# One transfer for four heads of q, and k and v of the first batch on all 128 partitions

## The chip, the cores and the metric

The kernel runs on one core of a Trainium2 chip. A core has five engines that each work through a queue of their own in order: TensorE (PE, matmuls; the loading of its weights is shown as PEld), VectorE (DVE), ScalarE (ACT), GpSimd (POOL) and SyncE (SP), which in this kernel issues all transfers. The metric is the device time of one execution in microseconds, and the kernel before and the changed one are compared by it.

## The reference

Linear attention feeds two layers with activations, the second with weights of its own; all data is float32.

```
q, k, v: [4 batches, 8 heads, 576 tokens, 64]
q_s = exp(q - max over 64), divided by its sum over the 64      # softmax over a head's width
k_s = exp(k - max over tokens), divided by its sum over tokens  # softmax over the 576 tokens
kv  = k_s^T v                  # 64 x 64 for each batch and head
x   = q_s kv                   # to [2304 tokens, 512]
h   = x @ w_in;  x2  = (h * sigmoid(1.702 h)) @ w_out           # 512 -> 2048 -> 512
h   = x2 @ w_in2; out = (h * tanh(softplus(h))) @ w_out2
```

## The kernel before

**Stages.** The tokens are cut into five blocks of 512, 512, 512, 384 and 384 (`SIZES`). For the first three blocks the first layer is done directly: for each of 16 column blocks of `w_in` a group of 12 matmuls makes `h` (`gemm_in`, L1029), ScalarE and VectorE make the activation `g` of it, and 12 matmuls add it to four accumulators `acc` (`gemm_out`, L1098). From 330 us on the rest of the first layer and the second one run as products of 256 to 384 columns with fewer multiplications (L1322, L1661, L1552). Each float32 operand is split into a high and a low part, so a product takes three matmuls (`SPLIT`). The 32 weight blocks of the first layer are loaded into four buffers `raw`, decoded on ScalarE and VectorE (L414 or L418, L450, L461, L474) and split (L404 or L405 for the high part, L397 for the low one) into `wi` and `wo`.

**Attention** is done block by block (`attention(blk)`). `q_soft` takes half of the heads: it loads four heads of q (for block 0 into `qr`, for later blocks into `qt` with `q_load`), and VectorE and ScalarE make the softmax. `q_turn` transposes two heads on TensorE (L918), a copy `qT` is taken (L928), and `x_part` multiplies it by the pair's `kv32` (L948); ScalarE and VectorE write the high and low part of x (`xt<-at`, L903 and L908). One `unit` is a pair of heads, and each batch has four. For the first batch it is `k_first`: TensorE turns k so that tokens lie along a row (L692), VectorE takes the maximum (L705), ScalarE the exponential with its sum (L720), TensorE turns it back (L731), a copy goes to `kt` (L740), and `k_kv` multiplies by v (L768). Later batches take `k_later`. In block 1 and later the units use the bank `at0`, and q and x the bank `at1`. k lies on 96 partitions with six tokens of each head (`KP`, `KC`):

```python
kt = [ap.tile([KP, 2, KC, D], F32, name=f"kt{i}") for i in range(2)]
vd += [sp.tile([KP, 2, KC, D], F32, name=f"vd{i}") for i in range(1, NHP)]
```

**Order.** Every piece of work is recorded as an operation with costs (`plan.op`), and `Plan` makes the order in which each engine's instructions are written. It plays the operations through by their costs with random noise on their urgency, `PASSES` times from `SEED`, and takes the best order. It also writes filler transposes of the identity (`idle`, L1696; 40 in the kernel before) where it sees TensorE idle ahead of the first matmul of h. So a changed cost or seed changes the order all through the program.

## Time and profile before

| | |
|---|---|
| median of 3 runs | 817.04 us (816.63 to 819.48) |
| the profiled execution | 817.37 us, of which its span 815.5 us |
| PE, DVE, ACT busy | 99%, 81%, 55% of the span |
| granted clock of TensorE | 1.000, the level of 2.4 GHz |
| transfers | 208.58 MB, 78.3% of 16 DMA engines' span |

The span runs from the first to the last instruction; launch and end lie around it. Matmuls are pipelined, so a busy PE counts time in which one waits inside the array as well.

### The profile page before, as it was taken

How to read it: one execution, taken by the hardware profiler on the slowest of the kernel's cores; microseconds unless marked ns; L12 is line 12 of the kernel's file. 1: busy time of each engine (PE TensorE's matmuls, PEld its weight loads, DVE VectorE, ACT ScalarE, POOL GpSimd, SP SyncE). 2: the span in 40 equal slices, each digit the busy share in tenths (PEclk: the TensorE clock that was granted, in tenths of full speed). 3: DMA queues.
4: the chain of work that ended last, by engine and by line, in shares of the span. 5: the costliest groups of instructions: out<-in, count | busy, mean ns of one | idle time of the engine just before them, and what ended most of it. 6: DMA issues, size and time to landing. Idle time of an engine off the chain costs nothing.

```text
span 815.5 us, 14362 instructions
## 1 busy us (share of the span) xinstructions
PE 806.4 (99%) x5104; PEld 734.5 (90%) x5104; DVE 657.9 (81%) x1272; ACT 452.2 (55%) x860; POOL 16.9 (2%) x22
## 2 busy tenths in 40 slices
PE   8999899999999999999999999999999999999998
PEld 7788678877788888999999999999999999999997
DVE  6999887799986787777779879978777996677963
ACT  5999765355665456655556545555344563344542
POOL 0000000010000001000000000002000010000000
PEclk9999999999999999999999999999999999999999
DMA  9799765457878788887798898999589897777752
GB/s 241 227 274 294 228 216 171 169 171 231 228 249 286 237 277 279 272 333 267 264 305 288 278 331 285 295 319 392 173 273 295 291 309 223 227 250 265 270 190 60
DMA packets 126984, 208.58 MB, mean 256 GB/s; under 512 B 37568, under 2 KB 87488, under 8 KB 126912
## 3 DMA queue, kind: packets, MB, share of 16 engines
q1 hardware_dynamic: 126912, 207.66, 78.3%
q8 instruction: 41, 0.67, 0.3%
q14 instruction: 31, 0.25, 0.1%
HBM read 152.57 MB, written 55.05 MB: 255 GB/s over the span
## 4 chain that ended last, share of the span: by engine, by line
PE 87%; DVE 2%; ACT 1%; DMA 1%; issue 0%; ACTq 0%; SPq 0%; DVEq 0%
PE acc L1552 22%; PE at L1322 18%; PE acc L1098 13%; PE h L1029 12%; PE h L1322 10%; PE acc L1661 5%; PE h L1661 2%; PE at L948 2%; PE at L768 1%; PE at L918 1%; DMA raw<-in_moe_w_out_dram 1%; DVE dec L474 0%; PE h L1552 0%; DVE dec L397 0%; ACT dec L450 0%
## 5 line engine op out<-in xcount | busy, mean ns | idle before, releaser
L1098 PE MATMUL acc<-g,wo 128*128 128x512 f32 x576 | 145.7, 396 | 0.0
L1029 PE MATMUL h<-xt,wi 128*128 128x512 f32 x576 | 144.7, 396 | 0.0
L1552 PE MATMUL acc<-wi,second 128*128 128x256 f32 x1116 | 137.5, 283 | 0.0
L1552 PEld LDWEIGHTS acc<-wi,second 128*128 128x128 f32 x1116 | 135.6, 192 | 0.0
L1098 PEld LDWEIGHTS acc<-g,wo 128*128 128x128 f32 x576 | 106.6, 188 | 23.0 <-issue 1.0
L1029 PEld LDWEIGHTS h<-xt,wi 128*128 128x128 f32 x576 | 106.2, 188 | 23.0 <-issue 1.1
L1322 PE MATMUL at<-xt,wi 128*128 128x384 f32 x612 | 119.1, 335 | 0.1
L1322 PEld LDWEIGHTS at<-xt,wi 128*128 128x128 f32 x612 | 106.8, 188 | 3.0 <-DVE gt L1374 0.4
L1344 ACT ACTIVATE quad<-quad 128x384 f32<-128x384 f32 x96 | 50.3, 526 | 89.1 <-DVE quad L1374 88.7
L405 ACT ACTIVATE second<-quad 128x384 fp32r<-128x384 f32 x125 | 64.8, 523 | 49.2 <-PE acc L1552 44.7
L397 DVE TENSOR_TENSOR second<-quad,second 128x384 fp32r<-128x384 f32 x126 | 71.4, 571 | 14.8 <-ACT second L405 14.3
L1322 PE MATMUL h<-xt,wi 128*128 128x384 f32 x348 | 66.0, 334 | 0.0
L397 DVE TENSOR_TENSOR quad<-quad 128x384 f32<-128x384 f32 x96 | 53.1, 556 | 13.9 <-ACT quad L1344 12.2
L1322 PEld LDWEIGHTS h<-xt,wi 128*128 128x128 f32 x348 | 60.8, 188 | 0.0
L1552 PE MATMUL acc<-wi,g 128*128 128x256 f32 x372 | 48.2, 283 | 0.0
L1322 PE MATMUL at<-wi,wi 128*128 128x384 f32 x246 | 48.2, 334 | 0.0
L1552 PEld LDWEIGHTS acc<-wi,g 128*128 128x128 f32 x372 | 46.2, 192 | 0.0
L474 DVE CUSTOM_DVE_ANT_0 dec<-raw,dec 128x1024 uint16<-128x1024 uint16 x64 | 43.7, 686 | 2.0 <-ACT raw L414 0.5
L405 ACT ACTIVATE raw<-dec 128x512 fp32r<-128x512 f32 (+1 forms) x61 | 35.4, 598 | 16.5 <-DVE dec L397 10.7
L1322 PEld LDWEIGHTS at<-wi,wi 128*128 128x128 f32 x246 | 43.3, 188 | 0.7
L405 ACT ACTIVATE g<-gt 128x512 fp32r<-128x512 f32 (+1 forms) x42 | 26.3, 626 | 30.9 <-PE acc L1098 29.0
L1052 ACT ACTIVATE gt<-h 128x512 f32<-128x512 f32 x41 | 24.4, 594 | 32.4 <-PE h L1029 32.1
(179 smaller groups left out, 1179.2 us busy)
## 6 DMA issues: line engine op xcount, KB each, us to landing
wi<-combos SPq DMA_DIRECT2D x96, 512.0 KB, 5.1
wi<-outs SPq DMA_DIRECT2D x76, 512.0 KB, 5.6
raw<-in_moe_w_in_dram SPq DMA_DIRECT2D x32, 512.0 KB, 5.2
raw<-in_moe_w_out_dram SPq DMA_DIRECT2D x32, 512.0 KB, 4.8
combos<-raw SPq DMA_DIRECT2D x32, 512.0 KB, 3.6
outs<-raw SPq DMA_DIRECT2D x32, 256.0 KB, 3.2
wi<-combos SPq DMA_DIRECT2D x32, 256.0 KB, 4.9
combos<-raw SPq DMA_DIRECT2D x24, 256.0 KB, 3.8
```

What stands on the lines that cost most here:

```text
L397: return lambda: engine.tensor_tensor(out=out(), in0=in0(), in1=in1(), op=op)
L405: (ACT, act_ns(n), lambda: nc.scalar.activation(out=out(), in_=in_(), func=AF.Copy), False),
L474: dve(512, [rl], [da], lambda: nc.vector.tensor_tensor(out=a, in0=a, in1=lo_w, op=ALU.add), pair=True)
L768: nc.tensor.matmul(out=ps3[j * D : (j + 1) * D, 0:width], lhsT=of[:, j, c, :], rhs=w[:, j, c, :], start=c == 0, stop=c == KC - 1,)
L948: nc.tensor.matmul(out=part(ps[:, 0:nb]), lhsT=kv32[hp], rhs=part(qT32[hp % 2][:, 0:nb]), start=True, stop=True)
L1029: nc.tensor.matmul(out=h(), lhsT=w_mm(fc, 0, a, cc), rhs=x_of(t)[:, cc, b, :], start=cc == 0 and i == 0, stop=cc == NCC - 1 and i == 2,)
L1052: act(nb, [hk, ("tables",)], [tk], lambda: nc.scalar.activation(out=t, in_=h, func=AF.Tanh, scale=0.851), psum=True)
L1098: nc.tensor.matmul(out=acc[dm][:, 0:nb], lhsT=w_mm(fc, 1, a, dm), rhs=g_of(n)[:, b, :], start=fc == 0 and i == 0, stop=fc == NFC - 1 and i ...
L1322: nc.tensor.matmul(out=bank_of(key)[:, 0:NB], lhsT=wt(fc, 0)[:, w : w + P], rhs=operand(k, b)[:, cc, :], start=cc == 0 and i == 0, stop=cc ...
L1344: nc.scalar.activation(out=t(), in_=t(), func=AF.Mish if n >= NPR else AF.Gelu_apprx_sigmoid)
L1552: nc.tensor.matmul(out=bank_of(banks[c])[:, at_ : at_ + 256], lhsT=slot(pr, a)[:, c * P : c * P + P], rhs=rhs(b), start=pr == 0 and i == 0 ...
L1661: nc.tensor.matmul(out=o, lhsT=w_mm(2 * n + j, 1, a, dm), rhs=g_tile(n, j)[:, b, lo:hi], start=n == 0 and j == 0 and i == 0 and (c < 4 or ...
```

## The change

k and v of the first batch lie on 128 partitions, 64 for each of the two heads, with nine tokens on each; the products of a unit of the first batch work on 64 by 64 tiles, 18 instead of 12 of them, and turning back is a matmul with the identity, no transpose. For block 1 and later, `q_load` issues one transfer for four heads where it issued four (the pieces of 256 bytes stay). The planner's costs, seed and number of passes change, and so do the places of some combinations of weights in the second half (`EARLY`, `LATE_RIGHTS`, `LATER`, `RIGHTS`, `FIRST`).

```diff
-    PASSES = 30
-    SEED = 2
+    PASSES = 20
+    SEED = 948
...
-    FREE = {DMA: 1700.0, POOL: 2200.0, PE: 1750.0}
+    FREE = {DMA: 2500.0, POOL: 2200.0, PE: 1750.0}
...
-    TURNS = ((0, 4), (4, 6))
+    HC = 9
+    HP = S // HC
+    TURNS = ((0, 6), (6, 9))
...
-    kt = [ap.tile([KP, 2, KC, D], F32, name=f"kt{i}") for i in range(2)]
+    kfull = [ap.tile([P, 2 * KC * D], F32, name=f"kt{i}") for i in range(2)]
+    kt = [t[0:KP, :].rearrange("p (j c d) -> p j c d", j=2, c=KC) for t in kfull]
...
+    kd = [t[:, 0 : HC * D] for t in kfull]
+    kd += [sp.tile([P, HC * D], F32, name=f"kt{i}") for i in range(2, NHP)]
...
+    def by_head(a, hp):
+
+        return a[0, 2 * hp : 2 * hp + 2].rearrange("h (p c) d -> (h p) (c d)", c=HC)
...
                 for c in range(lo, hi):
                     for j in range(2):
+                        o = slice(j * D, (j + 1) * D)
                         nc.tensor.matmul(
-                            out=ps[i][j * D : (j + 1) * D, (c - lo) * KP : (c - lo + 1) * KP],
-                            lhsT=t[:, j, c, :],
-                            rhs=ident[0:KP, 0:KP],
+                            out=ps[i][o, (c - lo) * HP : (c - lo + 1) * HP],
+                            lhsT=t[o, c * D : (c + 1) * D],
+                            rhs=ident[o, o],
...
-                    nc.tensor.transpose(
-                        ps[i][0:KP, (c % 3) * P : (c % 3 + 1) * P], turned[h][:, n * KP : (n + 1) * KP], ident
-                    )
...
+                        nc.tensor.matmul(
+                            out=ps[i][o, c * D : (c + 1) * D],
+                            lhsT=turned[i][o, c * HP : (c + 1) * HP],
+                            rhs=ident[o, o],
...
-            for j in range(4):
-                dma(
-                    (hi - lo) * 256,
-                    begun,
-                    [("qt", j, i)] if len(cuts) > 1 else q_keys([j]),
-                    lambda j=j, lo=lo, hi=hi: qt[lo // NCT : hi // NCT, :, j, :],
-                    lambda j=j, b=b, s=s, n=hi - lo: q[b, 4 * half + j, s : s + n, :].rearrange("(p c) d -> p c d", c=NCT),
-                    slow=2,
-                )
+            dma(
+                (hi - lo) * 1024,
+                begun,
+                [("qt", j, i) for j in range(4)] if len(cuts) > 1 else q_keys(range(4)),
+                lambda lo=lo, hi=hi: qt[lo // NCT : hi // NCT],
+                lambda b=b, s=s, n=hi - lo: q[b, 4 * half : 4 * half + 4, s : s + n, :].rearrange(
+                    "h (p c) d -> p c h d", c=NCT
+                ),
+                slow=1.5,
+            )
```

In the changed kernel the lines stand 4 to 23 lower: L692, L731, L768, L1696 and L1029 are L700, L740, L780, L1719 and L1052 there; L397, L404, L418, L461, L474 and L908 are L401, L408, L422, L465, L478 and L931; L414, L450, L903 and L928 are L418, L454, L926 and L951.

**TensorE at the start of the program, the first two units.** A row is a run of equal instructions; `kt_116` and `kt_117` are k of the first two pairs, `stage` the exponentials, `h_107<-ident` fillers. Before:

```order
L1696 MATMUL h_107<-ident 128x128 x18
L692 MATMUL acc_99<-ident,kt_116 64x96 x8
L692 MATMUL acc_100<-ident,kt_116 64x96 x4
L692 MATMUL acc_101<-ident,kt_117 64x96 x8
L692 MATMUL acc_102<-ident,kt_117 64x96 x4
L1696 MATMUL h_107<-ident 128x128 x5
L731 MATMUL acc_99<-ident,stage 96x128 x3
L731 MATMUL acc_100<-ident,stage 96x128 x3
L1696 MATMUL h_107<-ident 128x128 x7
L768 MATMUL acc_99<-gt,kt_116 64x64 x12
```

Now:

```order
L1719 MATMUL h_107<-ident 128x128 x12
L700 MATMUL acc_99<-ident,kt_116 64x64 x12
L700 MATMUL acc_100<-ident,kt_116 64x64 x6
L1719 MATMUL h_107<-ident 128x128 x4
L700 MATMUL acc_102<-ident,kt_117 64x64 x6
L700 MATMUL acc_101<-ident,kt_117 64x64 x12
L1719 MATMUL h_107<-ident 128x128 x24
L740 MATMUL acc_99<-ident,stage 64x64 x12
L740 MATMUL acc_100<-ident,stage 64x64 x6
L740 MATMUL acc_102<-ident,stage 64x64 x6
```

Each product has half as many instructions again, the way back to tokens goes from 6 to 18, and the longest run of fillers now stands between turning k and turning it back.

**VectorE between the second and the fourth x part of block 0** (`xt<-at` is the low part of x; `wi_69` and `wi_70` are the second and third tile of `w_in`). Before:

```order
L908 TENSOR_TENSOR xt<-at_112,xt 128x512
...
L805 TENSOR_SCALAR kv_3_123<-acc_101,rs 64x64
L397 TENSOR_TENSOR wi_69<-dec_93,wi_69 128x512
L675 TENSOR_TENSOR pmt<-pmt 96x128
L418 TENSOR_SCALAR raw_91<-raw_91 128x512
L675 TENSOR_TENSOR pmt<-pmt 96x128
L908 TENSOR_TENSOR xt<-at_111,xt 128x512
L474 ISA dec_94<-raw_90,dec_94 128x1024
L461 TENSOR_SCALAR dec_92<-dec_92 128x512
L908 TENSOR_TENSOR xt<-at_112,xt 128x512
L404 CAST wi_70<-dec_94 128x512
```

Now:

```order
L401 TENSOR_TENSOR wi_69<-dec_93,wi_69 128x512
L682 TENSOR_TENSOR pmt<-pmt 96x128
L422 TENSOR_SCALAR raw_91<-raw_91 128x512
L682 TENSOR_TENSOR pmt<-pmt 96x128
L422 TENSOR_SCALAR raw_88<-raw_88 128x512
L465 TENSOR_SCALAR dec_94<-dec_94 128x512
L478 ISA dec_94<-raw_90,dec_94 128x1024
L408 CAST wi_70<-dec_94 128x512
L422 TENSOR_SCALAR raw_89<-raw_89 128x512
L401 TENSOR_TENSOR wi_70<-dec_94,wi_70 128x512
L931 TENSOR_TENSOR xt<-at_111,xt 128x512
L931 TENSOR_TENSOR xt<-at_112,xt 128x512
```

The third tile of `w_in` is now decoded to its end, and two later raw tiles are begun, ahead of the third and fourth x part. Over the whole list ahead of the fourth x part (rows not shown here) the counts are: L401 for `wi` three for two, L408 two for none, L422 four for two, L465 three for four, and none for two of L805, whose work ScalarE does now.

**ScalarE in block 1, from the first copy of qT to the x part that follows** (`raw` are weights that a transfer brings, `wo_437` and `wo_541` the last four tiles of `w_out`). Before:

```order
L928 ACTIVATE qT_0_124<-at_112 128x512
L414 ACTIVATE raw_88<-raw_88 128x512
L450 ACTIVATE dec_93<-raw_88 128x512
L414 ACTIVATE raw_89<-raw_89 128x512
L450 ACTIVATE dec_94<-raw_89 128x512
L797 ACTIVATE kv_0_120<-at_111,rs 64x64
L903 ACTIVATE xt<-at_112 128x4x16
```

Now:

```order
L951 ACTIVATE qT_0_124<-at_112 128x512
L409 ACTIVATE wo_541<-dec_92 128x512
L454 ACTIVATE dec_94<-raw_89 128x512
L768 ACTIVATE kt_116<-kt_116 96x768
L926 ACTIVATE xt<-at_112 128x4x16
```

One conversion of a raw weight stands there for four, and the exponential of the block's first k pair has come in. On TensorE the two rows ahead of this and the work behind it read now as follows; before, the row of `mcol` and the product with `vt` (L752 and L768) stood far ahead of the q turn and just ahead of it:

```order
L941 MATMUL at_112<-ident,qt 128x128 x4
L765 MATMUL at_111<-ident,mcol 96x128
L1121 MATMUL acc_99<-g,wo_83 128x512 x3
L1121 MATMUL acc_100<-g,wo_83 128x512 x3
L971 MATMUL at_112<-qT_0_124,kv_0_120 128x4x16
L1121 MATMUL acc_101<-g,wo_83 128x512 x3
L1121 MATMUL acc_102<-g,wo_83 128x512 x3
L790 MATMUL at_111<-vt,kt_116 64x66 x12
L941 MATMUL at_112<-ident,qt 128x128 x4
```

SP's queue now holds all raw loads of the first layer ahead of the loads of block 1's second half of q; before, the last raw load stood behind them.

## Rows read from the trace of the kernel before

**Rows 1.** The chain that ended last, shares by engine.

```profile
PE 87%; DVE 2%; ACT 1%; DMA 1%; issue 0%; ACTq 0%; SPq 0%; DVEq 0%
```

**Rows 2.** Stretches (us): length, each engine busy (instructions), clock, DMA share, GB/s.

```profile
5.50:30.60 25.10, 24.13 (x277) 19.64 (x277) 23.64 (x53) 20.17 (x49) 0.00 (x0) 1.00 0.98 254
...
85.00:96.00 11.00, 8.63 (x62) 6.40 (x62) 9.25 (x21) 9.48 (x20) 1.44 (x1) 1.00 0.83 219
...
340.00:815.50 475.50, 471.36 (x3178) 462.36 (x3176) 364.66 (x702) 232.44 (x448) 7.35 (x4) 1.00 0.80 269
```

**Rows 3.** PE's waits, 34 to 340 us: total, times, longest.

```profile
PE at L918 <- DVE xt L908: 1.7, 1, 1.7
PE at L948 <- ACT qT L928: 0.6, 1, 0.6
```

**Rows 4.** PE in order of time, 28 to 36 us: start, length, run.

```profile
32.52 3.69 PE L1029 MATMUL h<-xt,wi 128*128 128x512 f32 x15
```

**Rows 5.** All engines in order of time, 0 to 40 us.

```profile
5.51 1.22 DVE L859 TENSOR_REDUCE qs<-qr 128x16 f32<-128x1024 f32 x1 [5.51 <-DMA qr<-in_q_dram]
...
6.58 4.11 PE L692 MATMUL acc<-ident,kt 96*64 96x96 f32 x48 [0.97 <-DMA kt<-in_k_dram]
...
11.22 0.82 PE L731 MATMUL acc<-ident,stage 128*96 128x128 f32 x6
...
12.73 0.92 PE L768 MATMUL acc<-gt,kt 96*64 96x64 f32 x24
...
14.92 1.21 PE L692 MATMUL acc<-ident,kt 96*64 96x96 f32 x24
...
29.89 0.68 DVE L908 TENSOR_TENSOR xt<-at,xt 128x512 fp32r<-128x512 f32 x1
```

**Rows 6.** Stretches of one microsecond, columns as in the second group.

```profile
3.00:4.00 1.00, 1.00 (x7) 1.00 (x6) 0.00 (x0) 0.00 (x0) 0.00 (x0) 1.00 1.04 357
...
13.00:14.00 1.00, 1.00 (x28) 0.93 (x23) 1.00 (x3) 1.00 (x5) 0.00 (x0) 1.00 1.09 257
```

**Rows 7.** PE's instructions of the units: ns (min/median/max, or busy us and mean).

```profile
L692 PE MATMUL acc<-ident,kt x96: 246/332/421, 6.6 to 19.2; 96*64 96x96 f32 x96
...
L731 PE MATMUL acc<-ident,stage 128*96 128x128 f32 x24 | 3.4, 276 | 0.0
L768 PE MATMUL acc<-vd,kt 96*64 96x64 f32 x72 | 2.7, 225 | 0.0
```

**Rows 8.** VectorE's instructions by shape, 0 to 34 us: busy us, mean ns.

```profile
L397 DVE TENSOR_TENSOR wi<-dec,wi 128x512 fp32r<-128x512 f32 x3 | 2.0, 667 | 0.0
...
L461 DVE TENSOR_SCALAR dec<-dec 128x512 int32<-128x512 int32 x5 | 2.1, 417 | 0.0
...
L418 DVE TENSOR_SCALAR raw<-raw 128x512 int32<-128x512 uint32 x3 | 1.3, 418 | 0.0
...
L805 DVE TENSOR_SCALAR kv<-acc,rs 64x64 f32<-64x64 f32 x2 | 0.6, 292 | 0.2
...
L404 DVE CAST wi<-dec 128x512 fp32r<-128x512 f32 x1 | 0.4, 412 | 0.0
```

**Rows 9.** ScalarE in order of time, 66 to 96 us.

```profile
71.51 0.83 ACT L755 ACTIVATE kt<-kt 96x768 f32<-96x768 f32 x1
...
88.64 0.58 ACT L928 ACTIVATE qT<-at 128x512 f32<-128x512 f32 x1
89.11 0.67 ACT L414 ACTIVATE raw<-raw 128x512 int32<-128x512 uint32 x1
...
91.42 0.68 ACT L414 ACTIVATE raw<-raw 128x512 int32<-128x512 uint32 x1 [1.09 <-DMA raw<-in_moe_w_out_dram]
...
92.75 0.21 ACT L903 ACTIVATE xt<-at 128x64 fp32r<-128x64 f32 x1
```

**Rows 10.** SP's issues in order of time, 84 to 97.5 us.

```profile
86.70 3.46 SPq L388 DMA_DIRECT2D qt<-in_q_dram  x4
...
96.93 0.52 SPq L388 DMA_DIRECT2D raw<-in_moe_w_out_dram  x1
```

More of the change, by code (lines that the diff above doesn't have):

```diff
@@ L443, in decoded @@
             src = w_ap[m][1][fc * P : (fc + 1) * P, :]
-        dma(P * 4096, pace, [rl, rh], lambda: dst, lambda: src, slow=1.2 if io == 0 else 1)
+        dma(P * 4096, pace, [rl, rh], lambda: dst, lambda: src, slow=1.15)
         if signed:
@@ L698, in turn @@
                         )
-            pe(180 * (hi - lo), [kk], [keys[i]], turn, whole=True)
+            pe(122 * (hi - lo), [kk], [keys[i]], turn, whole=True)
             dve(
-                (hi - lo) * KP,
+                (hi - lo) * HP,
                 [keys[i]],
                 [("km", u, i)],
-                lambda i=i, n=(hi - lo) * KP: nc.vector.reduce_max(out=km[:, u, i : i + 1], in_=ps[i][:, 0:n], axis=AX.X),
+                lambda i=i, n=(hi - lo) * HP: nc.vector.reduce_max(out=km[:, u, i : i + 1], in_=ps[i][:, 0:n], axis=AX.X),
             )
@@ L759, in k_kv @@
         kk = ("kt", k_tile(u))
-        t = kt[k_tile(u)]
-        width = D if first else D + 2
+        t = None if first else kt[k_tile(u)]
         def mm():
-            of = t.rearrange("p j c d -> p (j c d)").rearrange("p (c j d) -> p j c d", j=2, c=KC) if first else t
-            w = vd[u] if first else vt
+            if first:
+                for c in range(HC):
+                    for j in range(2):
+                        o = slice(j * D, (j + 1) * D)
+                        nc.tensor.matmul(
+                            out=ps3[o, 0:D],
+                            lhsT=kd[u][o, c * D : (c + 1) * D],
+                            rhs=vd[u][o, c * D : (c + 1) * D],
+                            start=c == 0,
+                            stop=c == HC - 1,
+                        )
+                return
             for c in range(KC):
@@ L777, in k_kv @@
         rk = ("rs", u % NHP)
-        pe(720, [kk] + [kk + (j,) for j in range(2)] + v_keys(u), [key3], mm, whole=True)
+        pe(1090 if first else 720, [kk] + [kk + (j,) for j in range(2)] + v_keys(u), [key3], mm, whole=True)
         if first:
```

60 lines of the change are left out of this document (31 added, 29 removed).

## The prediction

> **What bounds the kernel now.** I read the chain that ended last first: 87% of it is TensorE, and no other engine has more than 2% [rows 1]. Then the stretches [rows 2]: from 340 us on PE is busy for 471.36 of 475.50 us and the list of PE's waits is empty there, so whatever makes that part begin later or earlier moves the end by the same amount. Of all that lies between 34 and 340 us PE's waits name only two, 1.7 us for an x part on VectorE and 0.6 us for a qT copy on ScalarE, 2.3 us together [rows 3]; the stretch 85 to 96 us is where they lie (PE busy 8.63 of 11 us [rows 2]). So two places can give time: the opening, up to the moment when PE starts the groups of h without a break (it has 15 matmuls in one run from 32.52 us; the last 12 of them, the group of the third w_in tile, start 0.78 us on, at 33.3 us [rows 4]; such matmuls start 0.23 us apart, 15 in 3.69 us with the length of the last), and the two waits near 90 us, 2.3 us.
>
> In the opening VectorE is the engine that is full: it begins at 5.51 us, when the first half of q has landed, starts the fourth and last x part at 29.89 us [rows 5], and is busy for 23.64 of the 25.10 us between [rows 2]. PE is not full there: it runs 40 filler transposes of the identity.
>
> **The change part by part.** *The order of the first loads.* k of the first pair now stands ahead of q. Before, the first transposes of k wait until 6.58 us [rows 5], behind 512 KB of q and 288 KB of k. How fast the two move is in two rows: 357 GB/s in the microsecond that moves q (128 partitions), 257 in one that moves only k and v (96 partitions) [rows 6]. Without q ahead of it (524 KB / 357 = 1.5 us) and at the rate of q (295 KB: 1.15 us at 257, 0.83 at 357, so 0.3 less) k lands near 6.54 - 1.8 = 4.7 us. That does not start VectorE earlier: its first instruction is now the maximum over six transposed token blocks. The transposes of k from 6.58 us took 4.11 us for 48 records and those at 14.92 us 1.21 for 24 [rows 5]; less the length of the last record (0.42 at the most and 0.25 at the least [rows 7]) that is 0.15 and 0.08 us for a pair of records (two heads side by side), although the column of the granted clock says 1.00 (2.4 GHz) throughout. At the early pace 12 pairs of 64 columns take 12 x 0.15 x 64/96 = 1.2 us, so with 0.2 for the hand-over VectorE starts at about 6.1 us, 0.6 later than before.
>
> *128 partitions for k and v.* By the two rates eight transfers save 8 x 0.3 = 2.6 us of the DMA stream. [...] I take no gain from the faster transfers in the sum, since VectorE is full from 5.5 us and never starved by a landing after the first (bounds: 0 and -1.8 us, the earlier landing of k).
>
> *More matmuls for the same tokens.* A unit (pair of heads) has 18 instead of 12 in each of its products, and the way back is 18 matmuls where there were 6 transposes. Pairs of 64 columns: k times v has 24 records in 0.92 us [rows 5], of which the last alone is 0.22 [rows 7], so 0.058 us a pair; 18 matmuls are 18 such pairs, 1.05 us. Before: turning 12 x 0.08 = 0.98, back 6 x 0.109 = 0.65 (0.82 us for six [rows 5], less the last one's 0.27 [rows 7], over 5 spacings), k times v 0.70. So a unit costs PE 0.07 + 0.40 + 0.35 = 0.8 us more, four units 3.3. For the first two units the fillers in the row give way. For units 2 and 3 the way back and k times v, 2 x 0.75 = 1.5 us, stand between the first x part and the groups of h, where the built order has one filler instead of five, and PE has little else to give up.
>
> *VectorE's list ahead of the fourth x part.* In the built order it has one wi subtract (0.667), two casts (0.412) and two low-half conversions (0.418) more than before, and one shift (0.417) and two kv scalings (0.292) fewer [rows 8]: 0.67 + 0.82 + 0.84 - 0.42 - 0.58 = 1.3 us, or 1.0 since neighbours overlap by some 0.08 us each. This is decoding done ahead, not lost, but PE waits for the x part, not for it. ScalarE's second copy of a unit has 192 columns in place of 384; I count that as nothing, since the x part waits for VectorE's list.
>
> *Sum for the opening.* By VectorE: start +0.6, list +1.0, and it can win back at most the 1.46 us that it was idle: between +0.1 and +1.6 us, the middle +0.9. By PE: up to +1.5, less its one or two short gaps. Both say about **+1.0 us**; ends 0 and +2.1 (the upper if the early pace of PE outlasts the 24 fillers: 3.5 us more at half pace is 1.75 us of work on the way to kv of the first unit, of which the fillers hide some 0.7).
>
> *The two waits near 90 us.* Before, ScalarE has four conversions of raw weights between the first qT copy of block 1 (88.64 us) and the x part that frees PE's bank (92.75 us); one of them waits 1.09 us for its weights [rows 9]. The engine takes its queue in order, so the x part waits with it, and PE with the x part. Behind those weights four loads of q, a head each, hold the issuing queue for 3.46 us, and the last weights are only issued at 96.93 us [rows 10]. In the new order one raw conversion and the exponential of k stand between the qT copy and the x part, and all raw loads stand ahead of that half of q. From the end of the qT copy to that of the x part: a weight copy and a conversion at 0.6 each, k's exponential at 0.75 and the x part 0.2, together 2.15 us ([rows 9], less 0.08 of overlap each), while PE has the x product itself, 6 matmuls (1.36) and k times v (0.7): over 2.1 us. So the 1.7 should go and the 0.6 mostly: **-2.1 us**; ends -2.3 and, if the new chain waits as the old did, 0.
>
> *q in one transfer.* The pieces stay 256 bytes, so the bytes' time stays; 56 issues become 14. SP is no engine that PE waits for, and outside block 1 no wait on q is on PE's list [rows 3]: 0, with the gain at block 1 counted above. If one issue of four heads takes more than the four did (0.9 us each near 87 us [rows 10]), SP holds the next loads back; the blocks after the first have nothing near it that PE lacks. The rest of the reordering (pairing of weights, late combinations) I price at 0, between -0.5 and +0.5: PE has no wait there that could go.
>
> Sum: +1.0 - 2.1 = -1.1 us. The profiled execution took 817.37 us (span 815.50); less 1.1 is 816.3. Its time is 0.33 over the median of the runs, 817.04, so **815.9 us** by the median.
>
> **The rivals.**
> *The wait moves.* In the new order the maximum of block 1's first k pair comes back to PE only two rows after the q turn, and k must then pass VectorE (768 columns, at the pace of 1.22 us for 1024 [rows 5]: 0.9 us) and ScalarE (0.83 [rows 9], behind a weight that may not have landed) before k times v, six rows on. With three hand-overs at 0.15 that is 2.2 us; 12 matmuls (2.7 us) and an x product cover it. One landing as late as the 1.09 us of [rows 9], with VectorE late by a step too, and PE waits again, for k. Then 1 to 2 us of the 2.1 stay: 817 to 818, say 817.5. Against it: the loads are issued earlier.
> *The opening hangs on the landings.* If what VectorE does were paced by the transfers, k's 1.8 us earlier landing would pass through: -1.8 - 2.1 = 813.1. VectorE's 94% speaks against it. [...]
> *PE becomes the bound of the whole opening* and the change is slower: all 3.3 us of extra products are on the path, plus 0.6 of the late start, less the 2.1: 818.8; 821 if the wait moves too. It decides when PE has no filler left to give up in units 0 and 1; the 24 fillers in the new order (24 x 0.109 = 2.6 us at the later pace) speak against it, unless the early pace lasts beyond them.
> *Nothing is worth anything*: the opening as before and the waits as before, 817.0; it lies between the others.
>
> **How the numbers follow.** Forecast (815 to 817) 0.45; the wait moves 0.22; landings 0.13; PE the bound 0.15; nothing 0.05. Half a per cent, 4.1 us, is about what a measurement can tell from no change: faster is below 812.9, which takes the landings case and a little luck: 0.10; slower is above 821.1, PE the bound together with the wait: 0.06; the same 0.84. The range from 813.0 to 819.0 leaves out about one in six.
>
> **What would show it.** Right: the third tile's group of h starts at 34 to 34.5 us; VectorE's first instruction at about 6.1 us; k lands near 4.7; a unit's three products take 1.05 us each at full pace; PE's list of waits after 34 us sums to under 0.7 us. Wrong: h starting before 32.8 us (landings), after 35.5 us (PE), or a PE wait on ScalarE's k, on qT or on x in the 80s and 90s as large as before.

## The result: slower, 822.3 against 817.1 us

| | before | changed |
|---|---|---|
| median of 6 runs | 817.11 us (815.92 to 819.48) | 822.25 us (821.57 to 826.67) |
| ratio, 95% interval | | 1.0067 (1.0048 to 1.0086) |
| the profiled execution | 817.37 us, span 815.5 | 821.57 us, span 819.5 |

The changed kernel is 0.67% slower, outside the forecast's range. The page of the changed kernel, busy time of the engines and the chain that ended last:

```profile
PE 809.0 (99%) x5322; PEld 736.1 (90%) x5322; DVE 659.4 (80%) x1272; ACT 448.2 (55%) x854; POOL 20.2 (2%) x26
...
PE 71%; DMA 1%; DVE 1%; ACT 1%; issue 0%; SPq 0%; DVEq 0%; ACTq 0%
```

PE is still what the end hangs on, as in [rows 1]. Its waits from 30 to 340 us (line, what it waited for: total, times, longest):

```profile
PE at L790 <- ACT kt L768: 2.1, 5, 0.8
PE at L685 <- ACT kv L819: 0.6, 1, 0.6
PE at L941 <- ACT stage L915: 0.5, 1, 0.5
PE at L971 <- ACT kv L819: 0.4, 1, 0.4
PE at L971 <- DVE xt L931: 0.2, 1, 0.2
```

The two waits of [rows 3] are gone, but five lines with 3.8 us stand where there were 2.3. The stretches (columns as in [rows 2]), first from VectorE's first instruction to the end of its fourth x part:

```profile
5.27:31.30 26.03, 25.37 (x474) 20.89 (x469) 24.56 (x55) 20.99 (x51) 0.00 (x0) 1.00 0.85 271
```

```profile
85.00:96.00 11.00, 10.00 (x69) 7.52 (x68) 9.65 (x22) 8.95 (x19) 0.00 (x0) 1.00 0.89 244
...
340.00:816.00 476.00, 475.48 (x3200) 466.19 (x3198) 366.18 (x697) 237.14 (x459) 12.83 (x9) 1.00 0.81 270
```

Where the time went is read best by following the same matmul in both traces. Every kernel here has 576 matmuls of `h` in `gemm_in`, and counting them gives the same point of the work in each. The table compares the start of four matmuls with the profile of before, in us later (+) or earlier (-): number 25 of `h` (the third tile of `w_in`, 33.30 us before: end of the opening), number 193 (123.81: attention of block 1 is over), number 433 (253.64: attention of blocks 2 and 3 is over) and a late product of the first layer (717.52). "This" and "beside" are medians of timed runs, beside it the kernel before on the same chip.

| kernel | this | beside | ratio (95%) | opening | block 1 | block 2 | late |
|---|---|---|---|---|---|---|---|
| the changed kernel | 822.25 | 817.11 | 1.0067 (1.0048, 1.0086) | +1.09 | +1.03 | +4.19 | +4.31 |
| `after_again` | 822.82 | 816.91 | 1.0067 (1.0042, 1.0093) | +1.52 | +1.07 | +4.38 | +4.51 |
| `before_again` | 818.70 | 817.72 | 1.0007 (0.9987, 1.0028) | -1.91 | -1.87 | -1.31 | -1.31 |
| `b_q1` | 818.07 | 817.27 | 1.0008 (0.9993, 1.0023) | +1.37 | +1.78 | +1.93 | +1.94 |
| `b_kv128` | 819.94 | 817.27 | 1.0041 (1.0026, 1.0057) | +1.40 | +1.44 | +1.41 | +1.83 |
| `a_q4` | 832.92 | 817.27 | 1.0200 (1.0180, 1.0220) | +1.41 | +4.54 | +17.52 | +17.62 |
| `a_kv96` | 820.88 | 817.02 | 1.0043 (1.0027, 1.0059) | +1.57 | +1.12 | +2.34 | +2.44 |
| `a_qlate` | 824.57 | 817.27 | 1.0100 (1.0081, 1.0119) | +1.37 | +1.07 | +6.89 | +7.00 |
| `a_qlate2` | 823.00 | 817.02 | 1.0060 (1.0038, 1.0082) | +1.43 | +1.44 | +4.16 | +4.31 |
| `a_slow` | 821.37 | 817.72 | 1.0045 (1.0026, 1.0064) | +0.93 | +1.09 | +0.84 | +3.54 |
| `a_noload` | 818.85 | 817.15 | 1.0025 (1.0012, 1.0037) | +1.14 | +0.78 | +0.75 | +0.85 |
| `b_wait` | 816.78 | 817.02 | 0.9998 (0.9982, 1.0015) | +1.49 | +0.44 | +0.51 | +0.50 |
| `b_wait2` | 816.29 | 817.25 | 0.9995 (0.9981, 1.0009) | -1.34 | +0.28 | +0.31 | +1.28 |
| `b_kv128_fill` | 819.48 | 816.91 | 1.0036 (1.0022, 1.0050) | +1.29 | +1.59 | +1.58 | +1.78 |
| `b_fill` | 816.56 | 816.91 | 0.9996 (0.9984, 1.0008) | -0.74 | +0.05 | +0.06 | +0.07 |
| `a_fill` | 821.92 | 816.91 | 1.0062 (1.0042, 1.0081) | +0.61 | +1.02 | +4.91 | +5.03 |
| `a_seed` | 820.53 | 817.02 | 1.0032 (1.0013, 1.0052) | +0.01 | +0.55 | +3.49 | +3.80 |
| `b_seed` | 820.03 | 817.72 | 1.0035 (1.0013, 1.0057) | -1.04 | +2.45 | +2.44 | +3.54 |
| `b_q1_plan` | 820.64 | 817.72 | 1.0045 (1.0028, 1.0062) | -0.02 | +0.23 | +1.28 | +2.65 |

The first row is the answer: +1.1 us in the opening, nothing in block 1 (1.09 to 1.03), **+3.2 us in block 2**, +0.1 after it. The forecast had +1.0, -2.1, and 0 for all that follows.

### The profile page after: what moved, and what is told of

Same layout as the page of the kernel before. It is cut to its first block, busy times and chain, and to the rows that moved or that the text cites. A ratio compares the mean times of both kernels' runs of the same rounds, so it can differ in the third digit from the quotient of the medians.

```text
span 819.5 us, 14700 instructions
## 1 busy us (share of the span) xinstructions
PE 809.0 (99%) x5322; PEld 736.1 (90%) x5322; DVE 659.4 (80%) x1272; ACT 448.2 (55%) x854; POOL 20.2 (2%) x26
## 2 busy tenths in 40 slices
DMA packets 125799, 208.58 MB, mean 255 GB/s; under 512 B 36896, under 2 KB 85280, under 8 KB 125728
## 4 chain that ended last, share of the span: by engine, by line
PE 71%; DMA 1%; DVE 1%; ACT 1%; issue 0%; SPq 0%; DVEq 0%; ACTq 0%
PE acc L1575 22%; PE at L1345 18%; PE h L1345 10%; PE acc L1121 6%; PE acc L1684 5%; PE h L1052 5%; PE h L1684 3%; DMA raw<-in_moe_w_in_dram 1%; DMA combos<-raw 1%; PE at L971 0%; PE h L1575 0%; PE at L941 0%; PE at L790 0%; DVE dec L478 0%; DVE raw L401 0%
## 5 line engine op out<-in xcount | busy, mean ns | idle before, releaser
L1052 PE MATMUL h<-xt,wi 128*128 128x512 f32 x576 | 145.5, 396 | 0.0
L1052 PEld LDWEIGHTS h<-xt,wi 128*128 128x128 f32 x576 | 106.7, 188 | 23.4 <-issue 1.4
L401 DVE TENSOR_TENSOR second<-quad,second 128x384 fp32r<-128x384 f32 x126 | 73.2, 587 | 17.1 <-ACT second L409 16.6
L401 DVE TENSOR_TENSOR quad<-quad 128x384 f32<-128x384 f32 x96 | 53.0, 556 | 14.0 <-ACT quad L1367 12.4
L454 ACT ACTIVATE dec<-raw 128x512 f32<-128x512 f32 x62 | 41.3, 670 | 8.7 <-DMA raw<-in_moe_w_in_dram 6.1
L478 DVE CUSTOM_DVE_ANT_0 dec<-raw,dec 128x1024 uint16<-128x1024 uint16 x64 | 43.8, 686 | 0.8
```

Of the source, the lines that this page charges most:

```text
L401: return lambda: engine.tensor_tensor(out=out(), in0=in0(), in1=in1(), op=op)
L454: lambda: nc.scalar.activation(out=f32(a), in_=f32(hi_w), func=AF.Prelu, scale=2.0**-112, alpha=2.0**32),
L478: dve(512, [rl], [da], lambda: nc.vector.tensor_tensor(out=a, in0=a, in1=lo_w, op=ALU.add), pair=True)
L1052: nc.tensor.matmul(out=h(), lhsT=w_mm(fc, 0, a, cc), rhs=x_of(t)[:, cc, b, :], start=cc == 0 and i == 0, stop=cc == NCC - 1 and i == 2,)
```

## Experiments

Names that begin with `b_` start from the kernel before, those with `a_` from the changed one. Where the order is called that of before or of the changed kernel, the planner's costs and fillers are left as they were, so every engine's rows stand in that order and only the edit differs.

### Block 2: what the late q does

At 178.91 us VectorE's maximum of q waits for its transfer; k's subtraction stands behind it in VectorE's row, k's exponential behind that on ScalarE, and PE waits for it. The three engines of the changed kernel in order of time, first VectorE, then ScalarE, then PE:

```profile
178.91 1.22 DVE L882 TENSOR_REDUCE qs<-qt 128x16 f32<-128x1024 f32 x1 [0.64 <-DMA qt<-in_q_dram]
180.04 0.94 DVE L767 TENSOR_TENSOR kt<-kt,at 96x768 f32<-96x768 f32 x1
...
200.72 1.22 DVE L882 TENSOR_REDUCE qs<-qt 96x16 f32<-96x1024 f32 x1 [1.13 <-DMA qt<-in_q_dram]
...
219.25 1.22 DVE L882 TENSOR_REDUCE qs<-qt 96x16 f32<-96x1024 f32 x1 [1.25 <-DMA qt<-in_q_dram]
220.39 0.94 DVE L767 TENSOR_TENSOR kt<-kt,at 96x768 f32<-96x768 f32 x1
```

```profile
181.02 0.84 ACT L768 ACTIVATE kt<-kt 96x768 f32<-96x768 f32 x1 [2.19 <-DVE kt L767]
...
201.78 0.66 ACT L454 ACTIVATE dec<-raw 128x512 f32<-128x512 f32 x1 [1.96 <-DMA raw<-in_moe_w_in_dram]
...
221.36 0.84 ACT L768 ACTIVATE kt<-kt 96x768 f32<-96x768 f32 x1 [2.40 <-DVE kt L767]
...
227.67 0.66 ACT L454 ACTIVATE dec<-raw 128x512 f32<-128x512 f32 x1 [1.03 <-DMA raw<-in_moe_w_in_dram]
```

```profile
181.91 0.92 PE L790 MATMUL at<-vt,kt 96*64 96x66 f32 x24 [0.61 <-ACT kt L768]
...
204.90 0.91 PE L971 MATMUL at<-qT,kv 128*128 128x384 f32 x2 [0.45 <-ACT kv L819]
...
222.26 0.92 PE L790 MATMUL at<-vt,kt 96*64 96x66 f32 x24 [0.80 <-ACT kt L768]
...
229.16 0.55 PE L941 MATMUL at<-ident,qt 96*128 96x96 f32 x4 [0.52 <-ACT stage L915]
```

The same happens to k at 219.25 us. At 200.72 us the maximum waits 1.13 us and a kv scaling is late; but ScalarE, which works on q and kv there too, stands 1.96 us for a weight of `w_in` at the same time, and 1.03 us for another at 227.67, ahead of the `stage` that PE waits for at 229.16. Before, no maximum of q waits for q here, and ScalarE's longest wait for a weight in these blocks is 0.51 us. There is one `qt` tile, so a half of q can only be loaded once the second q turn of the half before has read it. In the changed kernel the turn starts at 171.59 us and the two transfers (one for each batch that the block touches) are issued in one run from 172.61 us:

```profile
172.61 1.51 SPq L392 DMA_DIRECT2D qt<-in_q_dram  x2
```

So what counts is the time from that turn to the maximum (us, with the part of it that the maximum waited for its data):

| half of q | before | changed | `b_q1` | `a_slow` |
|---|---|---|---|---|
| block 2, second | 7.96 | 7.32 (0.64) | 8.22 (0.19) | 8.88 |
| block 3, first | 7.69 | 6.96 (1.13) | 7.90 | 8.08 |
| block 3, second | 7.75 | 6.07 (1.25) | 8.36 (0.87) | 6.39 |

Less the waits the new order leaves 4.8 to 6.7 us, where the old one leaves 7.5 to 8.0 (0.27 of one went into a wait for another load). The landing itself varies: `a_slow` has one of 6.39 us with no wait.

**`b_q1`: the one transfer in the old order.** The four transfers of before become one, at the place of the fourth.

```diff
+            if together is None or issued[together] == 4:
+                nc.sync.dma_start(out=out(), in_=in_())
...
-                    lambda j=j, lo=lo, hi=hi: qt[lo // NCT : hi // NCT, :, j, :],
+                    lambda lo=lo, hi=hi: qt[lo // NCT : hi // NCT],
```

> The kernel before, its order of instructions untouched, with each four transfers of q made one at the place of the fourth. Theory A (the one transfer itself is late: it starts when the last of the four heads is free and lands 5 to 6 us after its issue, and VectorE's q maximum stands in the row ahead of k's subtraction): VectorE waits about 2 us for q at two or three places of block 2, PE waits 2 to 3 us more, 819 to 820 us. Theory B (the order made from another seed and other costs is what lost the time, and one transfer or four is the same to it): 816.5 to 817.8, no wait on q over 0.7 us.

1.0008 (0.9993 to 1.0023): no change that could be measured, though the median lies between the two ranges and the longer wait is over theory B's 0.7. VectorE waits for q here too (waits of VectorE, 85 to 240 us):

```profile
DVE qs L869 <- DMA qt<-in_q_dram: 1.1, 2, 0.9
```

But between block 1 and block 2 PE loses only 0.15 us (+1.78 to +1.93): at 216.89 us, where the longer wait is, k's subtraction has already run, at 213.48 us. So the one transfer by itself costs nothing that these runs can show (0.23% at the most); that the cost lies in what stands behind the maximum is how I read it.

**`a_q4`: four transfers in the new order.** At the place of each single transfer the four of before are issued.

```diff
+            for x, y in zip(o, a) if isinstance(o, list) else [(o, a)]:
+                nc.sync.dma_start(out=x, in_=y)
```

> The changed kernel, its order untouched, with four transfers of q, a head each, issued one behind the other at the place of the one. Theory A in its form 'one transfer lands later than four small ones': VectorE's three waits on q (0.6, 1.1, 1.3 us) shrink by half or more, 820 to 821 us. Theory A in its form 'it starts too late, when all four heads are free' and theory B (order): the waits stay or grow by up to the 2 us of three more issues each, 822 to 825 us.

2% slower. VectorE's waits for q grow from 3.0 to 6.9 us, and block 2 costs 13.0 us (+4.54 to +17.52). SP's queue and VectorE's waits:

```profile
94.87 5.48 SPq L394 DMA_DIRECT2D qt<-in_q_dram  x8
```

```profile
DVE qs L887 <- DMA qt<-in_q_dram: 6.9, 3, 3.3
```

Eight issues hold SP for 5.48 us in block 1, and block 1 costs 3.1 us too (+1.41 to +4.54). The new order needs the one transfer: with four in its place q is awaited longer still.

**`a_qlate` and `a_qlate2`: the maximum behind k.** In the new order the maximum of q is written behind k's subtraction (three places in `a_qlate2`, two in `a_qlate`, where the softmax of a third half goes behind kv instead).

```diff
+        ((('qmax', 1, 1),), (('ksub', 5),)),
+        ((('qmax', 2, 1),), (('ksub', 9),)),
+        ((('qmax', 3, 1),), (('ksub', 13),)),
```

> The changed kernel with three q maxima moved back in VectorE's row at the three places where VectorE waits for q in block 2 and 3: two of them behind k's subtraction that stood next, the third (with q's subtraction and exponential) behind the scaling of kv. Nothing else moves. If the wait on q, with k's and kv's work queued behind it, is what holds PE there: PE's waits at 181, 204 and 221 us (0.6, 0.45, 0.8 by the list, 2.3 with what shows as pauses) go, 819.8 to 820.5 us. If PE is held by something else that would be late next, under 0.5 us of gain: 821.8 to 822.5.

> The changed kernel with only q's maximum moved, at the three places where k's subtraction stands right behind it (second half of q of blocks 1, 2 and 3): behind that subtraction. The move of q's whole softmax behind kv, which gave VectorE's column maximum a wait of 3.0 us in the run before, is left out. If q's landing with k's subtraction queued behind it is a cause: 0.4 at 102, 0.5 to 0.8 at 181 and 0.8 us at 221 go, 820.2 to 821 us. If the time only moves to the next wait: 821.7 to 823.

Both took PE's waits for k at 181 and 222 us away, and neither was faster than the changed kernel. PE's longest waits in `a_qlate`, then in `a_qlate2`:

```profile
PE at L781 <- DVE mcol L702: 3.0, 1, 3.0
PE at L962 <- ACT stage L936: 1.8, 1, 1.8
```

```profile
PE at L962 <- ACT stage L936: 1.4, 1, 1.4
PE at L701 <- ACT kv L837: 0.6, 1, 0.6
```

In both, ScalarE waits 2.2 us for the weight near 201.8 us and about 2 us for a later one (at 230.39 and 227.65 us). In `a_qlate` VectorE's decoding stands 1.66 us behind the first, with q's moved softmax behind that, and the column maximum `mcol` is late by 3.0 us. `a_qlate2` still loses 2.7 us in block 2, of which 1.4 is the wait behind the second. So with the maximum out of the way the next late thing, a weight, holds the rows up.

**`a_slow`: the planner told of a later q.** The cost of the transfer is doubled, and the planner makes all of the order anew.

```diff
-                slow=1.5,
+                slow=3.0,
```

> The changed kernel with one number changed, the planner's cost of a q transfer (slow=3.0 for 1.5), so that the planner lets q land about 2 us later, near the 5.5 us from issue to landing that the trace of the changed kernel shows. If the loss of block 2 comes from q landing later than planned, with k's work in VectorE's row behind it: no wait of VectorE on q over 0.5 us, PE's waits under 2.5 us in 85 to 240 us, 819.5 to 820.5. If the new order is a draw as good or bad as any: waits at other places, 820.5 to 823.

Block 2's loss is gone (+1.09 to +0.84), with every load of q in place; no maximum waits for q, and ScalarE's longest wait for a weight there is 0.32 us. But the new order lost 2.7 us elsewhere, later: PE waits in it, from 340 us on (first line) and before (second):

```profile
PE h L1345 <- ACT raw L915: 1.7, 1, 1.7
```

```profile
PE at L971 <- ACT qT L951: 1.8, 1, 1.8
```

Since every row moved, this alone could not say that q was the cause.

**`a_noload`: no landing to wait for, every row kept.**

```diff
+            if not leave:
+                nc.sync.dma_start(out=out(), in_=in_())
...
+                leave=(blk, half) in ((2, 1), (3, 0), (3, 1)),
```

> The changed kernel with its order, in which three loads of q are left out: those of block 2's second half and of block 3's two halves (VectorE and ScalarE work on what the tile still holds, so the values of these rows are not the reference's; 1.5 MB of transfers less). Everything else stands as it stood. In the changed kernel the q tile is loaded again about 1 us after its second q turn (171.6, 193.8, 213.2 us) and the maximum stands 6.1 to 7.3 us behind that turn. Theory (the order puts q's maximum nearer to the turn than the one tile and the transfer allow, and all of block 2's loss follows from that): the three waits of VectorE for q, 3.0 us, go; TensorE's waits for k at 181 and 222 us and for kv at 204 us go; the loss from the end of block 1 to the end of block 2 against the kernel before falls from 3.2 us to under 1.0, of which 0.5 is the wait for raw weights near 229 us; about 819 us, ratio 1.002 to 1.004. Rival (the rows of the new order stand so close that the next late thing, a raw weight or a copy, takes the place of q): the waits for q go, but 2 us or more of the 3.2 stay; about 821.5 us, ratio 1.005 or more.

This kernel leaves out three loads of q and works on what the tile still holds; those rows of its output are not the reference's. The transfers shrink by 1.31 MB (208.58 to 207.27), not by the 1.5 of the expectation. Block 2's loss falls from 3.2 us to nothing (+0.78 to +0.75), and the time from 1.0067 to 1.0025 (1.0012 to 1.0037). PE's waits, 30 to 340 us:

```profile
PE at L794 <- ACT kt L772: 0.9, 2, 0.7
PE at L976 <- ACT qT L956: 0.4, 1, 0.4
PE at L976 <- DVE xt L936: 0.2, 1, 0.2
PE at L1350 <- ACT stage L920: 0.2, 1, 0.2
```

None of them lies in block 2's attention: from 160 to 236 us PE is busy for 75.86 of 76 us, against 73.34 in the changed kernel:

```profile
160.00:236.00 76.00, 75.86 (x497) 60.22 (x496) 68.33 (x148) 44.52 (x86) 2.83 (x3) 1.00 0.58 180
```

```profile
160.00:236.00 76.00, 73.34 (x481) 57.31 (x480) 66.43 (x144) 43.72 (x84) 2.82 (x3) 1.00 0.63 186
```

So the three loads are behind the loss. But the run takes two things away at once. Of ScalarE's waits for weights in these blocks (1.96, 0.57 and 1.03 us in the changed kernel) one is left:

```profile
205.70 0.67 ACT L458 ACTIVATE dec<-raw 128x512 f32<-128x512 f32 x1 [1.01 <-DMA raw<-in_moe_w_in_dram]
```

The weight awaited at 201.78 us is issued at 195.74, directly behind two transfers of q on SP's queue; without them it is issued at 193.62. So a load of q can cost by its own landing and by the weights behind it, and no run parts the two. Profiles with the same rows show both: `a_kv96` (below) loses only 1.2 us in block 2, with 1.5 us of waits for q on VectorE where the changed kernel has 3.0; `a_fill` loses 3.9 with 1.7 of them, and there PE's wait near 229 us is 1.7.

### Block 1: the waits near 90 us

**`b_wait`: the waits taken out of the old order.** Seven operations of the old order are written further back, so that the x part of [rows 9] stands ahead of the conversion that waits for its weights and the one behind it. `b_wait2` adds two more moves.

```diff
+    MOVES = (
+        ((307,), 434),
+        ((318, 317, 457), 436),
+        ((313, 314, 319), 437),
+    )
```

> The kernel before with eight instructions moved back by a few places in block 1: on ScalarE the last conversion of a raw weight pair and a kv scaling stand behind the x part, and a weight copy behind the qT copy; on VectorE three decode steps stand behind the low x part. Nothing else. If the two waits near 90 us are worth what the prediction took for them: PE's list of waits after 34 us is empty, -2.0 to -2.3 us, 814.8 to 815.3 us. If a wait of the same size follows (the rival that the wait moves, which is what the changed kernel shows in block 1): 816.3 to 817.3 us.

> b_wait with ScalarE's row in block 1 ordered further: the kv scalings stand directly behind the x part and ahead of the last conversion of a raw pair, and the qT copy of the second pair ahead of the two conversions that follow. If the waits near 90 us are a matter of rows: PE waits under 0.5 us there, 2 us less than the kernel before from the end of its opening on, a ratio of 0.997 to 0.998. If the landing of the last weights sets the pace of block 1 whatever stands in the row: again 1 us or less, 0.999 to 1.000.

`b_wait` gains 1.05 us in block 1 (+1.49 to +0.44), less than half of the 2.3, and the timed runs can't tell it from before. Its waits in place of the two of [rows 3]:

```profile
PE at L693 <- ACT kv L812: 0.7, 1, 0.7
PE at L963 <- ACT qT L943: 0.7, 1, 0.7
```

`b_wait2` moves two kv scalings and a qT copy forward as well. It has waits for qT of 1.4 and 0.5 us and one of 0.9 for `mcol` instead, enters block 1 at -1.34 and leaves it at +0.28. ScalarE waits for one of the last weights of `w_out` in all of them; the conversion that follows starts at 91.42 us before, 91.82 in `b_wait`, 91.36 in `b_wait2`:

```profile
91.36 0.68 ACT L431 ACTIVATE raw<-raw 128x512 int32<-128x512 uint32 x1 [1.28 <-DMA raw<-in_moe_w_out_dram]
```

In the changed kernel such a conversion starts at 93.50 us:

```profile
93.50 0.68 ACT L418 ACTIVATE raw<-raw 128x512 int32<-128x512 uint32 x1 [1.52 <-DMA raw<-in_moe_w_out_dram]
```

The new order leaves block 1 at +1.0 to +1.1 whether the opening was +0.61 (`a_fill`), +1.09 or +1.57 (`a_kv96`), with that conversion at 93.45 to 93.54 us in each; in `a_noload` it starts at 93.25 and block 1 ends at +0.78, in `a_qlate2` at 93.75 with +1.44, and in `a_q4`, after a wait of 2.05 us, at 97.03 with +4.54. In all eight profiles of this order block 1 ends 31.3 to 31.5 us behind that conversion; in seven of the old one (all but `b_kv128_fill`) 32.3 to 32.9 behind theirs. So the new order needs 1.0 us less after the conversion, and has it 2.1 us later, of which 1.1 is the opening. That fits an end of block 1 set by those weights, but no run moved their landing by itself.

### The opening

**`b_kv128` and `a_kv96`: the 128 partitions alone, and taken away.** Only the layout of the first batch's k and v and its products are changed in the old order, and put back in the new one.

```diff
-    vd = [gt2.rearrange("p i n -> p (i n)")[0:KP, 0:768].rearrange("p (j c d) -> p j c d", j=2, c=KC)]
+    vd = [gt2.rearrange("p i n -> p (i n)")[:, 0 : HC * D]]
```

> The kernel before, its order and its fillers untouched, with k and v of the first batch on 128 partitions. By the prediction's steps the 3.3 us of extra matmuls of the units and the later first maximum cost the opening 0 to 1.6 us and the new VectorE list of the changed order costs 1.0 apart from that: so here the third tile's group of h at 33.3 to 34.3 us, total 817 to 818. If the whole +1.06 us of the changed kernel's opening were the matmuls': 34.4 us and 818.1. If landings paced the opening: under 32.8 us. After 34 us nothing should differ.

> The changed kernel, its order and fillers untouched, with k and v of the first batch back on 96 partitions (six tokens, 12 matmuls a product, transposes back); q stays one transfer. Together with the run that gave q's merge no cost in the old order, this is the price of the new order alone against the kernel before. If the extra matmuls are the bound of the opening (the rival that PE becomes the bound): its opening ends 1.0 us or more sooner than the changed kernel's (third tile's group at 33.4 or less), total 819 to 820.5 us, and the loss of block 2 (3.1 us) stays. If VectorE's list of the new order is the bound, as predicted: opening as in the changed kernel, 34.2 to 34.6 us, total 821.5 to 822.5.

`b_kv128` is 0.41% slower (0.26 to 0.57). From VectorE's first instruction to the end of its fourth x part:

```profile
4.71:31.99 27.28, 26.74 (x497) 21.78 (x496) 23.63 (x53) 20.00 (x49) 0.00 (x0) 1.00 0.74 237
```

VectorE does what it did before (23.63 us busy) in 27.28 us instead of 25.10 [rows 2]: it idles for 3.65, and PE is full with 26.74. That looks as if PE had become the bound of the opening in this order, but the end of the opening (+1.40) is no later than that of `b_q1` (+1.37), which has the old layout, and fewer fillers did not bring it forward (below). What the 0.41% come from isn't shown. `a_kv96`, without the wider layout, ends its opening no earlier (+1.57), as it would if VectorE's list sets it; but its rows were planned for the new products. Its block 2 lost 1.2 us, not the 3.1 that I expected to stay.

**`before_again` and `after_again`: both kernels profiled once more.**

> The kernel before, once more, for a second profile of its opening: the third tile's group of h started at 33.30 us in the first profile, but at 34.67 and 34.79 us in two runs whose instructions up to there are the same (b_q1, b_wait). If 33.3 is the usual opening: 33.2 to 33.5. If it was an early one: 34.6 to 34.8, and the total by that much later.

> The changed kernel, once more. If its opening and its waits belong to the order: third tile's group at 34.3 to 34.8 us, and against the kernel before 0 us gained in block 1 and 2.7 to 3.3 us lost in block 2 (VectorE's waits on q at the same three places). If they fell so by chance: other places, or 1 us less or more.

The opening of the kernel before ended 1.91 us earlier this time. Its first transposes of k:

```profile
6.05 2.36 PE L693 MATMUL acc<-ident,kt 96*64 96x96 f32 x48 [0.43 <-DMA kt<-in_k_dram]
```

They took 4.11 us in [rows 5], the same 48 records, with a granted clock of 1.00 in both. `b_q1`, whose opening is the same code, ended it at +1.37. Five profiles of that opening (with `b_wait` and `b_wait2`) start the third tile at 31.39 to 34.79 us, so one of them says little. Six of the new one (`a_kv96` and `a_fill` aside) start it at 34.39 to 34.82: it is later by 1.4 us in the mean, and varies less. `after_again` repeats block 2's loss (3.3 us), with the same waits.

**`b_kv128_fill`, `b_fill`, `a_fill`: fewer fillers.** The last 17 of 40 are left out (12 of the 24 ahead of the way back in `a_fill`).

```diff
-                idle_matmul()
+                self.idles = getattr(self, "idles", 0) + 1
+                if not 23 < self.idles <= 40:
+                    idle_matmul()
```

> b_kv128 without its last 17 fillers (the runs of 7, 5, 1 and 4 behind the first units' work; 17 x 0.109 = 1.9 us of TensorE's row). If TensorE's row is what bounds the opening with 128 partitions (VectorE was idle for 3.65 of 27.28 us there): the fourth x part and the third tile's group come 1.2 to 1.9 us sooner, 33.0 to 33.5 us, and the total 818 to 818.7. If VectorE's list bounds it: no change, 34.5 to 34.8 us, 819.5 to 820.5. If TensorE falls to half pace without them: later, over 35 us.

> The kernel before without the same 17 fillers: the control. VectorE was idle for 0.39 of 23.74 us in the execution where TensorE reached its full pace early: there no gain is left, 31.2 to 34.8 us as the pace falls out, 816.5 to 818. If TensorE's row is on the path here too: median 1 us or more under the kernel before.

> The changed kernel with 12 of the 24 fillers that stand between turning k and turning it back (8.01 to 10.78 us, while the first exponentials are done at 10.2). If these fillers overrun the wait that they fill: the way back starts 0.6 to 0.8 us sooner and the third tile's group at 33.6 to 34.0 us, 821.3 to 821.8. If VectorE's list bounds the new order: 34.3 to 34.8 us and 822 to 823.

Nothing came of it in the time: each left block 1 as its parent kernel did, or within 0.15 us of it. In `a_fill` the third tile did start at 33.91 us, in the range for fillers that overrun and 0.5 us ahead of the six others, but that was gone by the end of block 1. In `b_kv128_fill` PE ran 1.4 us ahead until 18.5 us, and then paused for a reason that the profile doesn't show:

```profile
21.09 0.45 PE L745 MATMUL acc<-ident,stage 64*64 64x64 f32 x7 [1.49 <-issue]
```

So whether the fillers cost the wide layout anything stays open.

### Orders as draws

**`a_seed`, `b_seed`, `b_q1_plan`.** Each code with the other's seed, passes and `FREE`; and the kernel before with the new `q_load` alone, planned anew.

```diff
-    PASSES = 20
-    SEED = 948
+    PASSES = 30
+    SEED = 2
```

> The changed code with the old seed, number of passes and starting costs of the planner (2, 30 and 1700), so with an order of its own. If the loss in block 2 is a matter of the order that one seed gave, PE's waits in 85 to 240 us come out otherwise, anywhere from 1 to 8 us in sum, and the total lies apart from 822.2 by over 1 us; if it belongs to q in one transfer or to the new costs, VectorE waits for q at the same places and the sum is 3 to 4 us again.

> The code of the kernel before, with the changed kernel's seed, passes and starting costs of the planner (948, 20, 2500) and nothing else. If an order is a draw, and the kernel before has a lucky one: PE's waits after 34 us sum to 2 to 5 us, at other places than before, 818 to 822 us. If the loss belongs to the new q and k code: 816.5 to 817.8.

> The kernel before with the change's q load alone, as the change writes it (one operation with its own cost), and the planner with the old seed making a new order of it. The merged transfer pinned into the old order cost 0.7 us, not clear of zero. If orders are draws: another sum of waits, 818 to 821. If q in one transfer only frees SP, as the prediction has it: 816 to 817.8.

All three are 0.32 to 0.45% slower than before. `b_q1_plan` shows it best: the same edit that costs nothing measurable in the old order (`b_q1`) costs 0.45% in one that the planner makes for it. Each order has its own waits; `b_seed` has one for qT of 3.8 us:

```profile
PE at L948 <- ACT qT L928: 3.8, 1, 3.8
```

## Why the prediction was wrong

**The step that failed** is the one on q and on all that follows block 1: "q in one transfer ... 0", "the blocks after the first have nothing near it that PE lacks", and "the rest of the reordering ... at 0, between -0.5 and +0.5: PE has no wait there that could go". It was priced by the waits of the old order, and a list of waits tells what could go, not what could come. The transfer alone costs nothing measurable, that much was right (`b_q1`). But the order was made anew, with q's maximum at 6.1 to 7.3 us behind the turn that frees the tile instead of 7.7 to 8.0, and k behind it in VectorE's row. Block 2 lost 3.2 us, and `a_noload`, which kept every row and left three loads of q out, lost none of it. Of PE's waits there, 1.4 us are for k behind the late maximum, 0.45 for kv and 0.52 behind a weight; how much of the whole is q's own landing, and how much the weights that are issued behind q, stays open. The prediction took both landings as free, since the old order has no wait on them. The distance from turn to maximum could have been read beforehand: in the trace of before, and where the maximum stands now in the order. No rival had a new wait in block 2.

**The two waits near 90 us, -2.1: measured 0.** They did go, as forecast; PE is busy for 10.00 of the 11 us where it was for 8.63. The first rival happened in their place: k's exponential, kv and an x part are waited for, in the profile 0.26, 0.58, 0.27 and 0.22 us between 85 and 125 us. Those are 1.3 of the 2.3, and block 1 still ends as late as it began. The rest is no wait that the list names. Between the same two matmuls, before and in the changed kernel, PE idles 0.74 us less but is busy 0.71 us longer, for one record more:

```profile
65.97:123.81 57.84, 55.45 (x327) 42.88 (x326) 51.27 (x103) 43.26 (x81) 2.18 (x2) 1.00 0.79 241
```

```profile
67.03:124.84 57.81, 56.16 (x328) 43.17 (x327) 51.16 (x105) 39.66 (x76) 0.00 (x0) 1.00 0.78 229
```

So the list of waits is not the whole measure; what the added busy time is made of, the profile doesn't say. `b_wait` and `b_wait2` say the same of the old order: taking the named waits out is worth about 1 us of 2.3, or none. That the landing of the last weights holds the block is a reading of the profiles, not shown by a run.

**The opening, +1.0: measured +1.1 and +1.5 against the first profile of before**, and within it:
- VectorE's list: 24.56 us busy against 23.64 in [rows 2], +0.9, where +1.0 was worked out. Right.
- VectorE starts at 5.27 us, not 6.1: k had landed by 4.26, not 4.7 (the 6.54 that the sum started from stands in no row; PE's wait ends at 6.58). So it is 0.24 us earlier than before, not 0.6 later; with the longer list and the same 1.47 us of idle time its fourth x part ends 0.7 us later (31.30 for 30.60), and the third tile starts 1.1 later.
- A product of a unit runs in 1.22 us for 36 records in the profile, 1.05 by spacing. Right.
- "For the first two units the fillers in the row give way" failed. The 24 fillers run on after the exponentials of the first unit are there (10.3 us): they start at 8.01 us, and the way back follows them at 10.78. PE in order of time:

```profile
4.26 1.31 PE L700 MATMUL acc<-ident,kt 64*64 64x64 f32 x36
...
8.01 2.84 PE L1719 MATMUL h<-ident 128*128 128x128 f32 x24
10.78 1.61 PE L740 MATMUL acc<-ident,stage 64*64 64x64 f32 x48
```

That the sum came out against one profile of before is luck in part, since five profiles of that opening lie 3.4 us apart; the 1.4 us of the means bear it out better.

**The rivals.** "PE becomes the bound of the whole opening" is not settled: in `b_kv128` PE is full and VectorE idles, but fewer fillers gained nothing; in the new order PE (25.37 of 26.03 us) and VectorE (24.56) are both nearly full. "The opening hangs on the landings" is refuted: k landed earlier by more than forecast and the opening ended later. That the transfers of k and v run faster on 128 partitions, as the prediction took from the two rates in [rows 6], fits `b_kv128`: its transfers move 348 and 369 GB/s with the new pieces, against 264 and 271 in the same stretches of before:

```profile
5.00:10.00 5.00, 4.46 (x114) 3.91 (x115) 4.79 (x8) 2.16 (x6) 0.00 (x0) 1.00 1.00 348
10.00:15.00 5.00, 5.00 (x126) 4.53 (x123) 4.53 (x12) 4.34 (x12) 0.00 (x0) 1.00 1.06 369
```

That is 1.32 and 1.36 times as much; [rows 6] have 357 for 257, 1.39 times. These stretches carry weights too, and the pieces of k and v grew from 1536 to 2304 bytes, so no run shows how much the partitions make of it and how much the pieces. The faster transfers brought no time: `b_kv128` is slower.

**What stays open.** Of the 6.3 us between forecast (815.9) and measured time (822.25), 3.2 are block 2 and 2.1 the waits that were to go. The timed difference, 5.1 us, is larger than the 4.3 of the profiles; the opening of before differs by more than that gap from execution to execution, so I can't split it further. In `a_noload` 1.7 us (0.25%) stay, of which the profile has 0.85.

No version tried beats the kernel before: `b_wait`, `b_wait2` and `b_fill` have 1 well inside their intervals.

## What to carry to other kernels

When an edit makes a scheduler plan anew, price the new order and not only the edit: for each buffer that is used again, take the distance from the instruction that frees it to the first that needs its next contents, in the trace of before, and look up where the new order puts both, and what is issued behind that load. A wait that costs little in one order can cost more in another: VectorE waited 1.1 us for q in `b_q1`, where PE lost 0.15 us in block 2, and 3.0 us in the changed kernel, where k's work stood behind two of the three waits and block 2 lost 3.2. Before believing a gain or loss of a microsecond in an opening, profile the same kernel several times.

## What the runs showed of the hardware

PE's pace in the first microseconds differs between executions of the same code: the same transposes of k (48 records) took 4.11 us in the first profile of before and 2.36 in `before_again`, with a granted clock of 1.00 in the records of both. The profile gives that clock as a share and no frequency. At 1.00, the matmuls of 256, 384 and 512 columns in the profile of before (L1552, L1322, L1029) start 120, 173 and 227 ns apart in the median: 128 columns more take 53 and 54 ns, so 2.4 columns pass in a ns. With one column taken for each tick, that is an estimate of 2.4 GHz, the figure of the table and the prediction. A pause of 1.49 us on PE in `b_kv128_fill` has no releaser in the profile. And a transfer of four heads of q in pieces of 256 bytes took 5.3 us from issue to landing in the median of the changed kernel (3.9 to 6.6), against 2.9 (2.0 to 7.2) for one of the four that it replaces.
